# Transposing the normalized tokens of two chunks by DMA, adding the output bias on VectorE, and a new instruction order

## The chip, the cores and the metric

The kernel runs on one core of one Trainium2 chip. The metric is device time in microseconds of one execution, as the median of several runs. The profile that is read below is one execution of the same program; its span runs from the first to the last instruction, and the execution's own time is a little longer than its span.

## The reference, cut to what matters

Two layers read the same normalized tokens and their results are added to the input: a local attention with 32 heads of 20 channels, in which each token looks at itself and the seven tokens 2, 4, ... 14 places back, and a dense layer with a gelu in the middle.

```
x = A_x                              # 1 x 2048 x 640, bf16
xn = layernorm(x)
qkv = xn @ wqkv                      # 640 -> 3*640, heads of 20
logits[s, w] = q[s] . k[s - 2*w] / sqrt(20), w = 0..7   (masked below token 0)
A = (softmax(logits) applied to v[s - 2*w]) @ wo
B = gelu(xn @ w1 + b1) @ w2 + b2     # 640 -> 1536 -> 640
out = x + A + B
```

## The kernel before, in words

The 2048 tokens are cut into 4 chunks (n = 0 to 3) of 512 tokens, each of 4 blocks (bl) of 128 tokens. A chunk goes through these steps, named as in the planner:

- `st`, `rs`, `rc`: mean and variance of each token on VectorE, square root on ScalarE, reciprocal on VectorE.
- `xn`: the normalized block, 128 tokens x 640 channels, in one of 2 buffers. VectorE writes it for chunk 0, ScalarE for the others (L399).
- `tp`, `tc`: five 128x128 transposes of that block on TensorE into a PSUM tile of the pool `acc` (L417), and ScalarE's copy into the chunk's transposed tile `xnT` (L421), of which there are 3.
- `pj`, `pc` (for chunk 0 `gj`, `gc`): q, k and v by TensorE, and ScalarE's copies out of PSUM. `pad` copies 14 columns from the chunk before.
- `qk`, `lg`: eight products q*k shifted, on VectorE (L493), and their sums over each head's channels on TensorE (L505).
- `m`, `mx`, `ex`, `ss`, `ri`, `at`: the softmax, `ex` on ScalarE and the others on VectorE.
- `xd`, `xs`: the weights `attn` are spread to all channels (`ax`, one buffer) by two DMAs from SyncE and two from ScalarE (L572).
- `av`, `ad`, `ot`: eight products with v (L588), three sums (L597) and the last sum into `oT` (L603), on VectorE.
- `f1`, `ge`: the 12 tiles of the dense layer's first product on TensorE (L610) and the gelu on ScalarE (L621).
- `o`, `oc`, `od`: for each block five pieces on TensorE: pieces 0 to 3 multiply the gelu's tiles by `w2`, piece 4 multiplies `oT` by `wo`, all into the same two PSUM tiles `lo` (512 columns, L643) and `hi` (128 columns, L645). ScalarE copies them to one of 2 tiles `osb` (L650, L651), and a GpSimd DMA adds `osb` to the output in DRAM (L657).

The output in DRAM is first filled with x by one DRAM-to-DRAM DMA (L330). A GpSimd DMA then adds b2, broadcast to 128 rows (`b2bc`), to each block (L656), ahead of the block's own result. The last block is different: `xb` adds b2 to its x on VectorE (L427), a product with the identity adds that to PSUM, and its `lo` and `hi` parts are written without accumulation, from SyncE and from ScalarE (`oclo`, `ohi`, `ochi`).

PSUM tiles for `tp`, `pj`, `gj` and `f1` come from a pool of 4 (`acc`); so do `lo` and `hi` of every second block of the last chunk. The other blocks share one pair (`O`).

The order of the instructions is written out by a planner. Each step has an engine, a duration, a rank, the steps that it needs and the buffers that it holds. The planner plays this through in time: whenever an engine is free it starts the step with the lowest rank of those that are ready. The steps' functions are then called in the order of these starts, and each engine executes its instructions strictly in that order, waiting where the real data are late. DMAs are steps of a fourth engine, "dq", that does one at a time; the real queue is SyncE's. The table `RANK` holds offsets to the ranks, by the first three or four letters of a step's name.

```
early = base + (-37.0 if n == 1 else -85.0)          # base = n * 52
pl.add(f"pj{n}{which}{to}", PE, 1.08, r, ...)        # r = early, for v early + 20
pl.add(f"f1{n}{ft}", PE, 1.08, base + 10.0 + 1.0 * ft, ...)
pl.add(f"o{n}{bl}{pc}", PE, us, base + PERIOD + 8.0 + 8.0 * bl, ...)
pl.add("ohi", PE, 1.05, base + PERIOD + 90, ...)
```

Of the kernel before, what the change touches and what calls it, by code (L numbers as in the profile page):

```python
# [133 lines left out]
LASTB = S // P - 1  # L134
# [4 lines left out]


RANK = {
# [4 lines left out]
}  # L146


def make_plan(fns, offsets=RANK):

    pl = Plan(offsets)
# [6 lines left out]
    def f(kind, *a):  # L158
        return lambda: fns[kind](*a)

    def done(n, which):
        if n:
            return [f"pc{n}{which}{to}" for to in range(KT)]
        return [f"gc{bl}{g}" for bl in range(BPC) for g, parts in enumerate(GROUPS) if which in [p[0] for p in parts]]

    for n in range(NCH):
        base = n * PERIOD
        prev = base - PERIOD
        early = base + (-37.0 if n == 1 else -85.0)
        xnT, q, k, v, oT = (("xnT", n), ("q", n), ("k", n), ("v", n), ("oT", n))  # L170
# [10 lines left out]
            pl.add(f"rc{n}", VE, 0.25, early + -4.0, [f"rs{n}"], f("rstd", n, 0, BPC))  # L181
        for bl in range(BPC):
            xn, tp = ("xn", n, bl), ("acc", "tp", n, bl)
            pl.add(f"xn{n}{bl}", SE if n else VE, 0.65 if n else 0.42, early + -4.0 if n else -99, [f"rc{n}" if n else f"rc{n}{bl}"], f("xn", n, bl), [xn])
            pl.add(f"tp{n}{bl}", PE, 0.3, early + -3.0 if n else -99, [f"xn{n}{bl}"], f("tp", n, bl), [xn, tp])
            pl.add(f"tc{n}{bl}", SE, 0.65, early + -3.0 if n else -99, [f"tp{n}{bl}"], f("tc", n, bl), [tp, xnT])
        if n == NCH - 1:
            pl.add("xb", VE, 0.5, base + 36, [f"xn{n}{BPC - 1}"], f("xb"), after=31.0)

        if n == 0:  # L190
            for bl in range(BPC):
                for g, parts in enumerate(GROUPS):
                    ps, last = ("acc", "g", bl, g), max(p[0] for p in parts)
# [5 lines left out]
        for which, buf in enumerate((q, k, v)):  # L199
# [5 lines left out]
            if which:  # L205
                need = done(n - 1, which) if n else []
# [3 lines left out]
        L = ("L", n)  # L210
        for wp in range(W // 2):
            pr = ("prod", "qk", n, wp)
            for i in range(2):
                need = done(n, 0) + done(n, 1) + [f"pad{n}1"]
                pl.add(f"qk{n}{wp}{i}", VE, 1.42, base + 3.0 * wp + i, need, f("qk", n, wp, i), [q, k, pr])
            pl.add(f"lg{n}{wp}", PE, 0.6, n - 1000, [f"qk{n}{wp}{i}" for i in range(2)] + ([f"lg{n}{wp-1}"] if wp else []), f("lg", n, wp), [pr, L], slack=0.8)

        e, at, ax = ("e", n), ("attn", n), ("ax", n)
        m, rs, ss, z = ("m", n), ("rs", n), ("ss", n), ("prod", "z", n)
# [4 lines left out]
        pl.add(f"ri{n}", VE, 0.96, n - 1000, [f"ss{n}"], f("recip", n), [ss, rs])  # L224
        pl.add(f"at{n}", VE, 1.22, n - 1000, [f"ri{n}"], f("attn", n), [e, rs, at])
        pl.add(f"xs{n}", SE, 1.2, n - 1000, [f"at{n}"], f("xs", n), [at, ax])
        pl.add(f"xd{n}", DQ, 5.5, n - 1000, [f"at{n}"], f("xd", n), [at, ax])

        prs = [("prod", "av", n, wp) for wp in range(W // 2)]
        for wp in range(W // 2):  # L230
            for i in range(2):
                need = [f"xd{n}", f"xs{n}", f"pad{n}2"] + done(n, 2)
                pl.add(f"av{n}{wp}{i}", VE, 1.42, base + 15.0 + 6.0 * wp + i, need, f("av", n, wp, i), [v, ax, prs[wp]])
        for k2, (a, b, r) in enumerate(((0, 1, 9.0), (2, 3, 21.0), (0, 2, 22.0))):
            need = [f"av{n}{x}{i}" for x in (a, b) for i in range(2)] if k2 < 2 else [f"ad{n}0", f"ad{n}1"]
# [8 lines left out]
        for bl in range(BPC):  # L244
            ob = ("osb", n, bl)
            O = [("O", n, bl)] if n < NCH - 1 or bl % 2 == 0 else [("acc", "lo", n, bl), ("acc", "hi", n, bl)]
            final = n * BPC + bl == LASTB
            last = None
            for pc in range(5):
                need = [last] if last else [f"ge{n}{ft}" for ft in range(FT)] + (["xb"] if (n, bl) == (NCH - 1, BPC - 1) else [])  # L250
                if pc == 4:
                    need.append(f"ot{n}")
                us = (0.65, 0.65, 0.65, 0.87, 1.08)[pc] if final else (0.82, 0.82, 0.82, 0.82, 1.37)[pc]
                last = pl.add(f"o{n}{bl}{pc}", PE, us, base + PERIOD + 8.0 + 8.0 * bl, need, f("o", n, bl, pc, ("lo",) if final else ("lo", "hi")), O + (hTs if pc == 0 else hTs[3 * pc : 3 * pc + 3] if pc < 4 else [oT]), 31.0)
            if final:
                pl.add("oclo", SE, 0.55, base, [last], f("oclo"), O + [ob])
                last = pl.add("ohi", PE, 1.05, base + PERIOD + 90, [last], f("ohi"), O)
                pl.add("ochi", VE, 0.25, base, [last], f("ochi"), O + [ob])
                continue
            pl.add(f"oc{n}{bl}", SE, 0.78, base, [last], f("oc", n, bl), O + [ob])  # L260
            pl.add(f"od{n}{bl}", SE, 0.0, base, [f"oc{n}{bl}"], f("od", n, bl), [ob])
# [4 lines left out]
def kernel(  # L266
# [16 lines left out]
    nc = tc.nc  # L283
    assert tuple(A_x.shape) == (1, S, D) and tuple(B_w1.shape) == (D, F)

    x_sd = A_x.rearrange("b s d -> (b s) d")
    out_sd = out.rearrange("b s d -> (b s) d")
# [8 lines left out]
    xtp = ctx.enter_context(tc.tile_pool(name="xtp", bufs=3))  # L296
# [9 lines left out]
    x_sb = wts.tile([P, NCH * BPC, D], BF16, name="x_sb")  # L306
# [5 lines left out]
    b2bc = consts.tile([P, D], BF16, name="b2bc")  # L312
# [9 lines left out]
    for n in range(1, NCH):  # L322
        cs = slice(n * BPC, (n + 1) * BPC)
# [2 lines left out]
    nc.sync.dma_start(w2_sb[:], B_w2.rearrange("(t p) n -> p t n", p=P))  # L326
    nc.sync.dma_start(wo2[:], A_wo.rearrange("(p t) n -> p t n", t=KT))  # L327
    nc.sync.dma_start(b2bc[:], b2_bcast)  # L328

    nc.sync.dma_start(out_sd[0 : LASTB * P, :], x_sd[0 : LASTB * P, :])  # L330


    ident = consts.tile([P, P], BF16, name="ident")
# [31 lines left out]
    tiles = {}  # L365

    def get(key, make):
        if key not in tiles:
            tiles[key] = make()
        return tiles[key]  # L370
# [52 lines left out]
            tiles["tp", n, bl][:, 0 : KT * P].rearrange("p (t m) -> p t m", t=KT),  # L423
        )

    def do_xb():
        nc.vector.tensor_tensor(out=x_sb[:, LASTB, :], in0=x_sb[:, LASTB, :], in1=b2bc[:], op=ALU.add)  # L427


    def qkv_tile(n, which):  # L430
# [222 lines left out]
    def do_od(n, bl):  # L653
        b = n * BPC + bl
        rows = out_sd[b * P : (b + 1) * P, :]
        nc.gpsimd.dma_start(rows, b2bc[:], accum_op=ALU.add)  # L656
        nc.gpsimd.dma_start(rows, tiles["osb", n, bl][:], accum_op=ALU.add)  # L657


    last = (NCH - 1, BPC - 1)  # L660
# [18 lines left out]
    with tc.manual_schedule(engines=engines):  # L679

        idle = psA.tile([P, CH], F32, tag="acc", name="idle")
        for _ in range(WARM):
            nc.tensor.matmul(idle[:, 0:P], lhsT=ident[:], rhs=ident[:], start=True, stop=True)
        for t in make_plan(fns).run():
            t["fn"]()
# [30 lines left out]
```

## Time and profile before

| | |
|---|---|
| time, median of 3 runs | 227.08 us (226.92 to 228.39) |
| the profiled execution: its own time | 227.29 us |
| its span | 225.0 us |
| TensorE (PE) busy | 212.4 us, 94% |
| VectorE (DVE) busy | 175.3 us, 78% |
| ScalarE (ACT) busy | 115.7 us, 51% |
| GpSimd (POOL) busy | 27.8 us, 12% |
| mean granted TensorE clock | 0.995 |
| DMA traffic | 21.98 MB, mean 98 GB/s |

Names in the profile: PEld is TensorE's weight load; SPq, ACTq and POOLq are DMA issues from SyncE, ScalarE and GpSimd. A row of the timeline gives start and duration in us, engine, line, operation, output and inputs, the number of instructions, and in brackets the idle time of the engine before it and what ended it. Matmuls are pipelined: a row's duration reaches to the modelled end of its last one, so the cost of a run of matmuls is read from start to start.

### The profile page before, as it was taken

How to read it: one execution, taken by the hardware profiler on the slowest of the kernel's cores; microseconds unless marked ns; L12 is line 12 of the kernel's file. 1: busy time of each engine (PE TensorE's matmuls, PEld its weight loads, DVE VectorE, ACT ScalarE, POOL GpSimd, SP SyncE). 2: the span in 40 equal slices, each digit the busy share in tenths (PEclk: the TensorE clock that was granted, in tenths of full speed). 3: DMA queues.
4: the chain of work that ended last, by engine and by line, in shares of the span. 5: the costliest groups of instructions: out<-in, count | busy, mean ns of one | idle time of the engine just before them, and what ended most of it. 6: DMA issues, size and time to landing. Idle time of an engine off the chain costs nothing.

```text
span 225.0 us, 4057 instructions
## 1 busy us (share of the span) xinstructions
PE 212.4 (94%) x1728; PEld 123.2 (55%) x1754; DVE 175.3 (78%) x166; ACT 115.7 (51%) x203; POOL 27.8 (12%) x48
## 2 busy tenths in 40 slices
PE   6899999999996999999999999999999999999990
PEld 6799745555443555555555555555445455455550
DVE  3759997567399998999899999999998229995000
ACT  3675988887674746923277542221548431511220
POOL 2000004990000000101010001111100110101111
PEclk9999999999999999999999999999999999999998
DMA  6999992999300000227001422222200532202322
GB/s 228 366 368 389 378 468 42 155 171 198 92 0 0 3 0 0 32 39 179 0 3 26 97 92 29 29 32 31 32 0 0 109 110 29 29 3 29 54 29 35
DMA packets 13625, 21.98 MB, mean 98 GB/s; under 512 B 1144, under 2 KB 10744, under 8 KB 13560
## 3 DMA queue, kind: packets, MB, share of 16 engines
q1 hardware_dynamic: 7848, 14.52, 19.7%
q0 software_dynamic: 4320, 4.92, 16.9%
q10 hardware_dynamic: 1440, 2.29, 3.2%
q8 instruction: 13, 0.21, 0.4%
q14 instruction: 4, 0.03, 0.0%
HBM read 12.45 MB, written 7.54 MB: 89 GB/s over the span
## 4 chain that ended last, share of the span: by engine, by line
issue 71%; POOL 10%; SPq 9%; DMA 7%; POOLq 1%
DMA out_dram<-in_A_x_dram 7%; POOL out_dram L657 5%; POOL out_dram L656 5%; SPq L327 4%; SPq L324 2%; SPq L326 1%; SPq L325 1%; SPq L318 1%; SPq L321 0%; POOLq L711 0%; SPq L320 0%; SPq L328 0%; SPq L315 0%; POOLq L657 0%; POOLq L656 0%
## 5 line engine op out<-in xcount | busy, mean ns | idle before, releaser
L610 PE MATMUL hps<-xnT,w_sb 128*128 128x512 bf16 x234 | 55.2, 380 | 0.3
L588 DVE TENSOR_TENSOR pv<-vT,ax 128x2560 bf16<-128x2560 bf16 x32 | 45.9, 1485 | 12.2 <-DMA ax<-attn 12.1
L643 PE MATMUL lo<-w_sb,hT 128*128 128x512 bf16 x183 | 52.2, 380 | 0.0
L493 DVE TENSOR_TENSOR prod<-qT,kT 128x2560 bf16<-128x2560 bf16 x32 | 45.8, 1486 | 3.1 <-ACT kT L478 2.8
L621 ACT ACTIVATE hT<-hps,b1T 128x512 bf16<-128x512 f32 x48 | 31.9, 688 | 19.7 <-PE hps L610 14.4
L645 PE MATMUL hi<-w_sb,hT 128*128 128x128 bf16 x192 | 40.3, 219 | 0.6 <-issue 0.2
L610 PEld LDWEIGHTS <-w_sb 128*128 128x128 bf16 x240 | 22.4, 98 | 26.2 <-issue 1.5
L597 DVE TENSOR_TENSOR pv<-pv 128x5120 bf16<-128x5120 bf16 x12 | 33.8, 2822 | 0.2
L657 POOL DMA_DIRECT2D out_dram<-osb x15 | 12.9, 863 | 157.0 <-ACT osb L651 157.0
L650 ACT CAST osb<-lo 128x512 bf16<-128x512 f32 x15 | 8.8, 587 | 45.6 <-PE hi L645 29.6
L643 PEld LDWEIGHTS <-hT 128*128 128x128 bf16 x192 | 18.7, 98 | 22.5 <-issue 0.4
L643 PE MATMUL lo<-wo,oT 128*128 128x512 bf16 x76 | 22.4, 380 | 0.0
L645 PEld LDWEIGHTS <-hT 128*128 128x128 bf16 x192 | 18.3, 98 | 2.1
L656 POOL DMA_DIRECT2D out_dram<-b2bc x15 | 13.5, 2696 | 35.1 <-DMA out_dram<-in_A_x_dram 35.1
L443 PE MATMUL pps<-xnT,wq_sb 128*128 128x512 bf16 x72 | 17.5, 381 | 0.2
L443 PE MATMUL pps<-xnT,wk_sb 128*128 128x512 bf16 x74 | 17.3, 379 | 0.2
L645 PE MATMUL hi<-wo,oT 128*128 128x128 bf16 x80 | 16.9, 219 | 0.2
L443 PE MATMUL pps<-xnT,wv_sb 128*128 128x512 bf16 x72 | 16.7, 380 | 0.3 <-ACT xnT L421 0.2
L478 ACT CAST qT<-pps 128x512 bf16<-128x512 f32 x15 | 8.8, 588 | 11.5 <-PE pps L443 11.5
L505 PE MATMUL L<-prod,head_of 128*32 128x256 bf16 x320 | 11.7, 275 | 2.1 <-DVE prod L493 2.1
L376 DVE BATCH_NORM_STATS2 stats<-x_sb 128x6 f32<-128x320 bf16 x16 | 7.4, 462 | 7.1 <-DMA x_sb<-in_A_x_dram 7.1
L399 ACT ACTIVATE xn<-x_sb,nmr,rstd 128x640 bf16<-128x640 bf16 x12 | 10.8, 921 | 4.0 <-PE tp L417 4.0
(68 smaller groups left out, 217.2 us busy)
## 6 DMA issues: line engine op xcount, KB each, us to landing
w_sb<-in_B_w_dram SPq DMA_DIRECT2D x2, 1920.0 KB, 16.4
out_dram<-in_A_x_dram SPq DMA_DIRECT2D x1, 2400.0 KB
out_dram<-b2bc POOLq DMA_DIRECT2D x15, 160.0 KB, 7.3
out_dram<-osb POOLq DMA_DIRECT2D x15, 160.0 KB, 3.4
ax<-attn SPq DMA_DIRECT2D x8, 256.0 KB, 5.3
ax<-attn ACTq DMA_DIRECT2D x8, 256.0 KB, 6.6
x_sb<-in_A_x_dram SPq DMA_DIRECT2D x3, 640.0 KB, 11.4
wq_sb<-in_A_wqkv_dram SPq DMA_DIRECT2D x1, 800.0 KB, 4.7
```

Of the source, the lines that this page charges most:

```text
L399: nc.scalar.activation(xn[:], x_sb[:, b, :], ACT.Identity, bias=nmr[:, b : b + 1], scale=rstd[:, b : b + 1])
L443: nc.tensor.matmul(ps[:], lhsT=wqkv_p[which][:, ti, to, :], rhs=xnT[:, ti, :], start=(ti == 0), stop=(ti == KT - 1),)
L493: nc.vector.tensor_tensor(out=prod[:, i, :, :], in0=qkv_tile(n, 0)[:], in1=qkv_tile(n, 1)[:, :, off : off + CH], op=ALU.mult,)
L505: nc.tensor.matmul(L[j * H : (j + 1) * H, 2 * wp : 2 * wp + 2, :], lhsT=head_of[:], rhs=prod[:, :, t, j * P : (j + 1) * P], start=(t == 0 ...
L588: nc.vector.tensor_tensor(out=pv[:, i, :, :].rearrange("p t (j c) -> p t j c", j=BPC), in0=qkv_tile(n, 2)[:, :, off : off + CH].rearrange( ...
L597: nc.vector.tensor_tensor(out=ta[:], in0=ta[:], in1=tb[:], op=ALU.add)
L610: nc.tensor.matmul(ps[:], lhsT=w1_sb[:, ti, ft * P : (ft + 1) * P], rhs=tiles["xnT", n][:, ti, :], start=(ti == 0), stop=(ti == KT - 1),)
L621: nc.scalar.activation(hT[:], tiles["hps", n, ft][:], ACT.Gelu_apprx_tanh, bias=b1T[:, ft : ft + 1], scale=1.0)
L643: nc.tensor.matmul(lo[:], lhsT=lhs, rhs=rhs[:, 0:CH], start=first, stop=last)
L645: nc.tensor.matmul(hi[:, 0 : D - CH], lhsT=lhs, rhs=rhs[:, CH:D], start=first, stop=last)
L656: nc.gpsimd.dma_start(rows, b2bc[:], accum_op=ALU.add)
L657: nc.gpsimd.dma_start(rows, tiles["osb", n, bl][:], accum_op=ALU.add)
```

## The change

- The blocks of chunks 2 and 3 are no longer transposed on TensorE and copied by ScalarE. Each normalized block is transposed by one DMA from SyncE straight into `xnT` (`do_td`, a step of the engine "dq" with 4.0 us).
- The DRAM-to-DRAM copy of x and the GpSimd DMAs that add `b2bc` are gone. Instead VectorE adds b2 to the x of a whole chunk in one instruction of 128 x 2560 (`xb0` to `xb3`), and a DMA from SyncE writes the result to the output (without the last block). The `o` steps of a chunk need its `xb`.
- The offsets in `RANK` are others, and a few durations in the plan are changed, so the order is another.

```diff
 RANK = {
-    "ad01": -51.8, "ad02": -11.1, "ad22": 55.2, "av0": -75.4, "av1": -80.6, "av2": 15.4, "f10": 39.3, "f11": 0.8,
-    "f12": 46.1, "f13": 9, "ge1": -74.9, "gj3": 24.7, "o00": 64.8, "o01": 58, "o02": 58.8, "o21": 9.1,
-    "o30": 13.6, "o32": -88, "o33": -87.4, "pc10": 184.3, "pc12": -37.1, "pj21": -29.9, "qk1": -33.9, "qk2": -278.2,
-    "qk3": -4, "st2": 95.7, "tc1": -44.4, "tp2": 50.9, "tp3": -44.5, "xb": 57, "xn1": 17.4, "xn2": 19.4,
+    "ad00": 178, "av2": 376.9, "f11": 47.4, "f12": 101.9, "f13": 56.6, "gj1": 41.2, "gj3": 41.9, "o01": -41.2,
+    "o02": 33.3, "o13": 84.5, "o23": 46.4, "ot0": 75.1, "pc12": 58.9, "pj30": 33.5, "pj32": 57, "qk2": -89.4,
+    "st2": 250.4, "tc1": -2.9, "xb0": 48.2,
 }
...
-            pl.add(f"xn{n}{bl}", SE if n else VE, 0.65 if n else 0.42, early + -4.0 if n else -99, ...)
+            pl.add(f"xn{n}{bl}", SE if n else VE, 0.81 if n else 0.42, early + -4.0 if n else -99, ...)
+            if n > 1:
+                pl.add(f"tc{n}{bl}", DQ, 4.0, early - 3.0, [f"xn{n}{bl}"], f("td", n, bl), [xn, xnT])
+                continue
             pl.add(f"tp{n}{bl}", PE, 0.3, ...)
             pl.add(f"tc{n}{bl}", SE, 0.65, ...)
-        if n == NCH - 1:
-            pl.add("xb", VE, 0.5, base + 36, [f"xn{n}{BPC - 1}"], f("xb"), after=31.0)
+        pl.add(f"xb{n}", VE, 1.43, base + 36, [f"xn{n}{bl}" for bl in range(BPC)], f("xb", n), after=32.0)
...
-            pl.add(f"lg{n}{wp}", PE, 0.6, ...)
+            pl.add(f"lg{n}{wp}", PE, 0.65, ...)
-        pl.add(f"xd{n}", DQ, 5.5, ...)
+        pl.add(f"xd{n}", DQ, 6.0, ...)
...
-                need = [last] if last else [f"ge{n}{ft}" for ft in range(FT)] + (["xb"] if (n, bl) == (NCH - 1, BPC - 1) else [])
+                need = [last] if last else [f"ge{n}{ft}" for ft in range(FT)] + [f"xb{n}"]
...
-    nc.sync.dma_start(out_sd[0 : LASTB * P, :], x_sd[0 : LASTB * P, :])
...
-    def do_xb():
-        nc.vector.tensor_tensor(out=x_sb[:, LASTB, :], in0=x_sb[:, LASTB, :], in1=b2bc[:], op=ALU.add)
+    def do_td(n, bl):
+        xnT = get(("xnT", n), lambda: xtp.tile([P, KT, CH], BF16, tag="xnT", name="xnT"))
+        nc.sync.dma_start_transpose(xnT[:, :, bl * P : (bl + 1) * P], tiles["xn", n, bl][:])
+
+    def do_xb(n):
+        cs = slice(n * BPC, (n + 1) * BPC)
+        nc.vector.tensor_tensor(
+            out=x_sb[:, cs, :],
+            in0=x_sb[:, cs, :],
+            in1=b2bc[:].unsqueeze(1).to_broadcast([P, BPC, D]),
+            op=ALU.add,
+        )
+        cs = slice(n * BPC, min((n + 1) * BPC, LASTB))
+        nc.sync.dma_start(out_sd.rearrange("(b p) d -> p b d", p=P)[:, cs, :], x_sb[:, cs, :])
...
     def do_od(n, bl):
         b = n * BPC + bl
         rows = out_sd[b * P : (b + 1) * P, :]
-        nc.gpsimd.dma_start(rows, b2bc[:], accum_op=ALU.add)
         nc.gpsimd.dma_start(rows, tiles["osb", n, bl][:], accum_op=ALU.add)
```

More of the change, by code (lines that the diff above doesn't have):

```diff
@@ L183, in make_plan @@
             xn, tp = ("xn", n, bl), ("acc", "tp", n, bl)
-            pl.add(f"xn{n}{bl}", SE if n else VE, 0.65 if n else 0.42, early + -4.0 if n else -99, [f"rc{n}" if n else f"rc{n}{bl}"], f("xn", n, bl), [xn])
+            pl.add(f"xn{n}{bl}", SE if n else VE, 0.81 if n else 0.42, early + -4.0 if n else -99, [f"rc{n}" if n else f"rc{n}{bl}"], f("xn", n, bl), [xn])
+            if n > 1:
+                pl.add(f"tc{n}{bl}", DQ, 4.0, early - 3.0, [f"xn{n}{bl}"], f("td", n, bl), [xn, xnT])
+                continue
             pl.add(f"tp{n}{bl}", PE, 0.3, early + -3.0 if n else -99, [f"xn{n}{bl}"], f("tp", n, bl), [xn, tp])
             pl.add(f"tc{n}{bl}", SE, 0.65, early + -3.0 if n else -99, [f"tp{n}{bl}"], f("tc", n, bl), [tp, xnT])
-        if n == NCH - 1:
-            pl.add("xb", VE, 0.5, base + 36, [f"xn{n}{BPC - 1}"], f("xb"), after=31.0)
+        pl.add(f"xb{n}", VE, 1.43, base + 36, [f"xn{n}{bl}" for bl in range(BPC)], f("xb", n), after=32.0)
         if n == 0:
@@ L215, in make_plan @@
                 pl.add(f"qk{n}{wp}{i}", VE, 1.42, base + 3.0 * wp + i, need, f("qk", n, wp, i), [q, k, pr])
-            pl.add(f"lg{n}{wp}", PE, 0.6, n - 1000, [f"qk{n}{wp}{i}" for i in range(2)] + ([f"lg{n}{wp-1}"] if wp else []), f("lg", n, wp), [pr, L], slack=0.8)
+            pl.add(f"lg{n}{wp}", PE, 0.65, n - 1000, [f"qk{n}{wp}{i}" for i in range(2)] + ([f"lg{n}{wp-1}"] if wp else []), f("lg", n, wp), [pr, L], slack=0.8)
         e, at, ax = ("e", n), ("attn", n), ("ax", n)
@@ L226, in make_plan @@
         pl.add(f"xs{n}", SE, 1.2, n - 1000, [f"at{n}"], f("xs", n), [at, ax])
-        pl.add(f"xd{n}", DQ, 5.5, n - 1000, [f"at{n}"], f("xd", n), [at, ax])
+        pl.add(f"xd{n}", DQ, 6.0, n - 1000, [f"at{n}"], f("xd", n), [at, ax])
         prs = [("prod", "av", n, wp) for wp in range(W // 2)]
```

## The prediction

> **What bounds the kernel now.** I read the page's busy times first, then the busy times by stretch.
>
> ```profile
> span 225.0 us, 4057 instructions
> PE 212.4 (94%) x1728; PEld 123.2 (55%) x1754; DVE 175.3 (78%) x166; ACT 115.7 (51%) x203; POOL 27.8 (12%) x48
> ```
>
> ```profile
> 50.00:75.00 25.00, 22.67 (x159) 11.83 (x161) 19.39 (x13) 17.13 (x26) 0.53 (x1) 1.00 0.35 70
> 75.00:100.00 25.00, 24.59 (x189) 13.72 (x191) 24.07 (x17) 14.92 (x26) 0.86 (x1) 1.00 0.08 10
> ...
> 175.00:200.00 25.00, 24.84 (x148) 12.73 (x150) 16.90 (x11) 8.82 (x17) 2.59 (x3) 1.00 0.32 63
> ```
>
> In these rows the columns after the stretch's length are PE, PEld, DVE, ACT and POOL busy, then the granted clock. PE is busy for 24.59 to 24.84 of 25 us in six of the seven stretches from 25 to 200; in the other one (50 to 75) it idles for 2.33. A busy PE could still be a slow one, so I checked its pace in the timeline: 20 matmuls of 512 columns take 4.48 us, of which 0.38 is one matmul's whole duration, so (4.48 - 0.38) / 19 = 0.216 us each, and a tile of `f1` (five) 1.08 us. That pace holds wherever such runs stand.
>
> ```profile
> 174.35 4.48 PE L610 MATMUL hps<-xnT,w_sb 128*128 128x512 bf16 x20
> ```
>
> PE is therefore the bound from its first transpose to its last matmul. What a change is worth is (1) PE work that disappears, (2) PE idle time that disappears, and (3) the stretch after PE's last matmul.
>
> The one large idle time is found in the timeline, together with what made VectorE late:
>
> ```profile
> 37.05 13.49 POOL L656 DMA_DIRECT2D out_dram<-b2bc  x15 [35.09 <-DMA out_dram<-in_A_x_dram]
> 48.70 1.31 SPq L572 DMA_DIRECT2D ax<-attn  x2
> 59.87 8.50 DVE L588 TENSOR_TENSOR pv<-vT,ax 128x2560 bf16<-128x2560 bf16 x6 [4.11 <-DMA ax<-attn]
> 68.29 1.48 DVE L493 TENSOR_TENSOR prod<-qT,kT 128x2560 bf16<-128x2560 bf16 x1
> 69.83 0.73 PE L505 MATMUL L<-prod,head_of 128*32 128x256 bf16 x20 [2.06 <-DVE prod L493]
> 184.13 5.70 DVE L588 TENSOR_TENSOR pv<-vT,ax 128x2560 bf16<-128x2560 bf16 x4 [8.03 <-DMA ax<-attn]
> ```
>
> The first `ax` is issued at 48.70 and used at 59.87, 11.2 us later. The 15 DMAs that add `b2bc` are issued from 37.05 to 50.5, so they are in flight then. VectorE idles 4.11 us for `ax`; the product after these six is late by that, and PE waits 2.06 us for it.
>
> The end:
>
> ```profile
> 204.12 1.49 DVE L603 TENSOR_TENSOR oT<-pv 128x2560 bf16<-128x2560 bf16 x1
> 210.46 0.59 ACT L665 CAST osb<-lo 128x512 bf16<-128x512 f32 x1 [0.38 <-ACT osb L651]
> 211.07 0.35 SPq L666 DMA_DIRECT2D out_dram<-osb  x1
> 217.82 0.83 PE L645 MATMUL hi<-w_sb,hT 128*128 128x128 bf16 x12
> 218.54 0.44 PE L645 MATMUL hi<-wo,oT 128*128 128x128 bf16 x5
> 218.57 0.59 ACT L650 CAST osb<-lo 128x512 bf16<-128x512 f32 x1 [3.82 <-DMA out_dram<-osb]
> 219.40 0.36 ACTq L675 DMA_DIRECT2D out_dram<-osb  x1
> 219.62 0.86 POOL L657 DMA_DIRECT2D out_dram<-osb  x1 [3.71 <-ACT osb L651]
> ```
>
> ```profile
> out_dram<-osb POOLq DMA_DIRECT2D x15, 160.0 KB, 3.4
> ax<-attn SPq DMA_DIRECT2D x8, 256.0 KB, 5.3
> x_sb<-in_A_x_dram SPq DMA_DIRECT2D x1, 160.0 KB, 2.7
> out_dram<-osb SPq DMA_DIRECT2D x1, 128.0 KB, 3.1
> out_dram<-osb ACTq DMA_DIRECT2D x1, 32.0 KB, 1.5
> ```
>
> PE ends at 218.98 and the span at 225.0, 6.02 later. ScalarE's copy of the second last block waits for a free `osb` (3.82, until an accumulating DMA has landed), then GpSimd issues at 219.62; 3.4 us to landing gives 223.0, and 2.0 us of closing follow.
>
> **The change part by part.**
>
> *Transposes, chunks 2 and 3.* In the timeline these are the last eight groups of five at L417. I take each from its start to the next matmul's start:
>
> ```profile
> 64.88 0.72 PE L417 MATMUL tp<-ident,xn 128*128 128x128 bf16 x10
> 65.44 2.32 PE L610 MATMUL hps<-xnT,w_sb 128*128 128x512 bf16 x9
> 71.58 0.72 PE L417 MATMUL tp<-ident,xn 128*128 128x128 bf16 x10
> 72.14 0.38 PE L643 MATMUL lo<-w_sb,hT 128*128 128x512 bf16 x1
> 73.77 0.44 PE L417 MATMUL tp<-ident,xn 128*128 128x128 bf16 x5
> 74.26 1.24 PE L443 MATMUL pps<-xnT,wk_sb 128*128 128x512 bf16 x4
> 88.48 0.73 PE L417 MATMUL tp<-ident,xn 128*128 128x128 bf16 x10
> 89.05 0.38 PE L643 MATMUL lo<-wo,oT 128*128 128x512 bf16 x1
> 90.52 0.44 PE L417 MATMUL tp<-ident,xn 128*128 128x128 bf16 x5
> 91.11 1.24 PE L443 MATMUL pps<-xnT,wv_sb 128*128 128x512 bf16 x5 [0.15 <-ACT xnT L421]
> ```
>
> 0.56 + 0.56 + 0.49 + 0.57 + 0.59 = 2.77 us of PE, all of it on the bound. Without the short waits for ScalarE's copy (the 0.15 above, and what makes the single groups dearer than half of a pair) it is 8 x 0.28 = 2.2. I take **-2.8**, bounds -2.2 and -2.8. The eight copies that go from ScalarE lie beside PE's work (ACT 51%) and are counted at nothing.
>
> The Trainium skill, page "VectorE: DVE Perf Modes", section "The three transpose paths", puts a 128x128 transpose on TensorE at 390 ns. By it the 40 transposes would be worth 15.6 us and the kernel would come down to about 208 us. The trace shows 0.056 us each, start to start, so the measurement decides and the term stays at 2.8.
>
> ```profile
> 45.19 0.92 ACT L399 ACTIVATE xn<-x_sb,nmr,rstd 128x640 bf16<-128x640 bf16 x1
> ```
>
> *Eight DMA transposes on SyncE's queue.* None is in the trace. The nearest rows are the load of the same 160 KB, 2.7 us, and the SBUF-to-SBUF `ax` on the same queue, 5.3 us for 256 KB; the longest `ax` was the first one, 11.2 us from issue to use. I take 5.3, as the nearest row in both places and queue, with 2.7 and 11.2 as the ends. It adds two waits. TensorE's first projection of chunk 2 or 3 waits for the last transpose of that chunk, and everything on PE stands behind it; the trace normalizes chunk 2's first block at 45.19, while the first projection that reads it starts at 74.26, so some 29 us lie between against 4 x 5.3 = 21 if they run one by one. And `xn` has two buffers: on ScalarE the third block's `xn` waits for the first one's transpose, and so on, six such waits in all, with gelus and PSUM copies queued behind. The planner reserves 4.0 us for each, so at 5.3 a wait is 1.3 us. PE meanwhile has up to four `acc` tiles, 4 x 1.08 = 4.3 us of work. Cost at 5.3: **0**; if all six came in one run, 6 x 1.3 - 4.3 = 3.5. Behind a transpose that waits, SyncE's `ax` DMAs wait too; they are issued with VectorE's softmax, tens of us apart, and I count nothing.
>
> *Bias on VectorE.* An add of 128x2560 is priced by L603, 1.486 us; the single add of before goes:
>
> ```profile
> L603 DVE TENSOR_TENSOR oT<-pv 128x2560 bf16<-128x2560 bf16 x4 | 5.9, 1486 | 0.1
> L427 DVE TENSOR_TENSOR x_sb<-x_sb,b2bc 128x640 bf16<-128x640 bf16 x1 | 0.5, 486 | 0.0
> ```
>
> 4 x 1.486 - 0.486 = 5.46 us more on VectorE, which isn't the bound. It would become one if `oT` of the last chunk came too late. PE needs after that `oT` four pieces 4 (89.05 to 90.52 above: at most 1.47 each, 5.9) and pieces 0 to 3 of the one block that finds no PSUM before (12 pairs, 12/5 x 1.47 = 3.5): 9.4 us. Before, it had 13.4 (205.6 to 218.98). With PE ending at 214.1 (below), `oT` must be there at 204.7, 0.9 earlier than before and with 5.46 more work: VectorE must recover 6.4 us of its idle time. I see 4.1 in the first `ax` wait, whose cause goes (next part), and two adds, 3.0, that fit into waits: `xb3` ranks at 192, in the neighbourhood of the 8.03 us wait at 176. That is 7.1: enough, narrowly. Cost **0**.
>
> *Output DMAs.* The DRAM-to-DRAM copy and the 15 bias DMAs go; four writes of x come (640 KB each, 480 the last), spread over the run, issued from SyncE. The first `ax` then has no accumulations beside it, so the 4.11 us of VectorE and with them PE's 2.06 go: **-2.1**, bounds 0 (the new order puts a wait elsewhere, or a write of x stands ahead of an `ax` on the queue) and -2.3. The accumulation of a chunk's first block now waits for that chunk's write; two `osb` tiles cover it.
>
> *Order and tail.* Without the offsets on `o32` and `o33`, the ranks make `o33` (156 + 52 + 32 = 240) the last block, so its `lo`, then `hi`, end PE, and the accumulating blocks end at least a piece earlier. With T as PE's end: `hi` takes 1.16 (217.82 to 218.98); `lo` ends at T - 1.16, ScalarE starts 0.1 later, SyncE issues 0.61 after that (210.46 to 211.07), landing 3.1: T + 2.65, closing 2.0: T + 4.65, against T + 6.02 now: **-1.4**. Bounds: 0, and -2.1 if only the small write counts (T + 0.42 + 1.5 + 2.0).
>
> Sum: span 225.0 - 2.8 - 2.1 - 1.4 = 218.7, with PE ending at 218.98 - 2.8 - 2.1 = 214.1. The profiled execution took 227.29, 2.29 over its span, so 221.0 for its like; it lies 0.21 above the median of 227.08, which makes **220.8 us**.
>
> **The rivals.**
>
> *VectorE becomes the bound.* None of its `ax` waits is recovered: `oT` at 205.6 + 5.46 = 211.1, PE's end at 211.1 + 9.4 = 220.5, span 225.1, time 227.2. For it: DVE is busy 24.07 of 25 us from 75 to 100. Against it: 12.1 us of waits for `ax` in the two rows above.
>
> *Only the transposes count.* The stall moves and the end still hangs on an accumulation, so the searched order doesn't do what it says: 227.1 - 2.8 = 224.3. For it: nothing in the plan knows how long an accumulating DMA holds `osb`.
>
> *Slower: the transposes land late.* Place: the six `xn` on ScalarE. At 11.2 us each wait is 7.2 beyond the plan, less 4.3 of cover 2.9, six times 17.4: 238. If the six come together, so that PE's cover counts once, 6 x 7.2 - 4.3 = 38.9 would be the far end, and the point from which it decides falls from 4.0 + 4.3 + 6.3/6 = 9.4 to 4.0 + (4.3 + 6.3)/6 = 5.8 us. The planner spaces them, so I price it at 238 and go by 9.4. For it: nothing in this trace transposes by DMA. Against it: both nearest rows are under 5.4.
>
> The Trainium skill, in the section named above, gives 1309 ns for a 128x128 block through the DMA, an estimate of 6.5 us for five in a row; with the six excesses of 2.5 together and cover once that would be 220.8 + 15 - 4.3 = 231.5, and with the waits apart nothing. The Trainium skill, page "Advanced Engine Details and Errata", section "X-Bar Transpose (TRN2)", says that transposes are as fast as regular DMAs, which would leave the sum. No trace here shows a transpose by DMA yet.
>
> **How the numbers follow.** Forecast 0.60; VectorE bound 0.17; only the transposes 0.10; late transposes 0.13. 1% of this kernel is 2.3 us, about what its measurement can tell from no change. Faster by over 1% takes the forecast and most of the third case, 0.67; within 1% the second and the rest, 0.19; slower 0.14. The low end has all terms at their better bounds, 2.8 + 2.3 + 2.1, and half a us of PE's other idle time: 227.1 - 7.7 = 219.4, rounded down to 218.5 since the other stretches idle for up to 0.41 each. The high end holds the second case and a mild form of the last: 228.5.
>
> **What would show it.** PE's busy time 2 to 3 us lower; no PE wait over 1 us between 25 and 200; transposes landing under 6 us; the first `ax` used within 7 us of its issue; PE's end near 214 and the span's 4 to 5 later, after a write from SyncE. It is wrong if ScalarE's `xn` waits for transposes by several us and PE for PSUM behind it, if PE waits for `oT`, or if the writes of x delay `ax`.

## The result and the profile after

The changed kernel takes **218.65 us** (median of 4 executions, 218.45 to 218.93); the kernel before took 227.74 (226.92 to 230.62) beside it. The ratio is 0.961, with a 95% interval of 0.957 to 0.966: 3.9% faster, where I had forecast 2.8%; 218.65 lies just inside the low end of my range, 218.5. (The ratio leaves out the 230.62, a disturbed execution.) The changed kernel's profiled execution took 218.45, its span 216.7; against that of before (227.29 and 225.0) the span is 8.3 us shorter and the time 8.8.

First the page of the changed kernel (busy times), then its busy times by stretch, with the same columns as before.

```profile
span 216.7 us, 3977 instructions
PE 209.4 (97%) x1689; PEld 121.1 (56%) x1714; DVE 180.2 (83%) x169; ACT 110.6 (51%) x195; POOL 14.5 (7%) x33
```

```profile
50.00:75.00 25.00, 24.54 (x171) 12.44 (x174) 24.93 (x17) 16.29 (x25) 0.00 (x0) 1.00 0.45 109
75.00:100.00 25.00, 24.89 (x163) 13.34 (x164) 24.86 (x18) 13.27 (x23) 1.88 (x2) 1.00 0.28 68
...
175.00:200.00 25.00, 24.84 (x162) 13.33 (x165) 17.15 (x10) 6.33 (x14) 3.44 (x4) 1.00 0.17 21
```

PE's busy time fell by 3.0 us (212.4 to 209.4). The stretch from 50 to 75, where PE had idled for 2.33, now has 0.46 of idle time. (Part of the small idle times may be records that the profile lacks: it has 1689 matmuls for 1714 weight loads here, and 1728 for 1754 before. The kernel with TensorE's transposes back, below, has 1754 of each, and there PE is busy for 25.00 us in each of the four stretches from 100 to 200.) VectorE's busy time rose by 4.9, and it is nearly full from 50 to 100 (24.93 and 24.86); but from 175 on it has 8 us to spare, as before.

The timeline of the changed kernel around the stall of before, and where VectorE stands at the end:

```profile
34.77 2.89 DVE L432 TENSOR_TENSOR x_sb<-x_sb,b2bc 128x2560 bf16<-128x2560 bf16 x2
48.79 1.29 SPq L584 DMA_DIRECT2D ax<-attn  x2
56.76 8.49 DVE L600 TENSOR_TENSOR pv<-vT,ax 128x2560 bf16<-128x2560 bf16 x6
69.05 0.73 PE L517 MATMUL L<-prod,head_of 128*32 128x256 bf16 x20
198.11 1.49 DVE L615 TENSOR_TENSOR oT<-pv 128x2560 bf16<-128x2560 bf16 x1 [7.35 <-PE hi L657]
```

The six products that read `ax` start at 56.76 with no wait in brackets (before: 59.87, after 4.11 of waiting), and PE's logits at 69.05 have none either (before: 2.06). The last `oT` waits 7.35 us *for PE* (`oT` has one buffer, and PE's products still read it): VectorE is early, not late.

The DMA issues of the changed kernel (the last column is the median time to landing), and, from the answers for the tiles `xnT` and `ax`, the range of the landings of each, with that of `ax` in the kernel before as the third:

```profile
ax<-attn SPq DMA_DIRECT2D x8, 256.0 KB, 4.9
xnT<-xn SPq DMA_TRANSPOSE x8, 2.6
out_dram<-osb SPq DMA_DIRECT2D x1, 128.0 KB, 1.7
out_dram<-osb ACTq DMA_DIRECT2D x1, 32.0 KB, 1.5
```

```profile
DMA to landing us min/median/max: 2.6/2.6/5.6
```

```profile
DMA to landing us min/median/max: 4.0/5.3/7.0
```

```profile
DMA to landing us min/median/max: 4.0/5.9/10.3
```

```profile
58.56 0.92 ACT L398 ACTIVATE xn<-x_sb,nmr,rstd 128x640 bf16<-128x640 bf16 x1 [1.25 <-DMA xnT<-xn]
```

A block's DMA transpose lands in 2.6 us in the median (5.6 at most), half of what I had taken, and only one of the six `xn` that could wait for a transpose does so, for 1.25 us. The longest landing of an `ax` fell from 10.3 to 7.0 (the 11.2 of the prediction runs from the first issue to the use).

The end, in the timeline of the changed kernel:

```profile
211.04 0.86 POOL L668 DMA_DIRECT2D out_dram<-osb  x1 [3.76 <-ACT osb L663]
213.12 0.44 PE L657 MATMUL hi<-wo,oT 128*128 128x128 bf16 x5
213.25 0.36 SPq L677 DMA_DIRECT2D out_dram<-osb  x1
213.98 0.36 ACTq L686 DMA_DIRECT2D out_dram<-osb  x1
```

PE ends at 213.12 + 0.44 = 213.56 and the span 3.14 later (before: 6.02). The last accumulation is issued at 211.04, before PE's end; what ends the run is the small write of ScalarE at 213.98, which lands 1.5 later, at 215.5, and 1.2 us of closing.

So the span's 8.3 us are 5.4 of PE's end (218.98 to 213.56: 3.0 of busy time, 2.4 of idle time) and 2.9 of tail. A further 0.5 lies outside the span, 2.29 before and 1.75 after.

### The profile page after: what moved, and what is told of

The parts are those of the page before. It is cut to its first block, busy times and chain, and to the rows that moved or that the text cites. A ratio compares the mean times of both kernels' runs of the same rounds, so it can differ in the third digit from the quotient of the medians.

```text
span 216.7 us, 3977 instructions
## 1 busy us (share of the span) xinstructions
PE 209.4 (97%) x1689; PEld 121.1 (56%) x1714; DVE 180.2 (83%) x169; ACT 110.6 (51%) x195; POOL 14.5 (7%) x33
## 3 DMA queue, kind: packets, MB, share of 16 engines
q10 hardware_dynamic: 1440, 2.29, 3.1%
## 4 chain that ended last, share of the span: by engine, by line
PE 93%; DVE 1%; ACT 1%; DMA 1%; ACTq 1%; issue 1%; DVEq 0%
PE lo L655 27%; PE pps L455 23%; PE hps L622 22%; PE gps L472 8%; PE hi L657 8%; PE L L517 5%; DMA x_sb<-in_A_x_dram 1%; PE tp L416 1%; ACTq L584 1%; ACT L633 1%; DVE stats L375 0%; DVE stats L376 0%; ACT xnT L420 0%; ACT hT L633 0%; DVE xn L402 0%
## 5 line engine op out<-in xcount | busy, mean ns | idle before, releaser
L622 PE MATMUL hps<-xnT,w_sb 128*128 128x512 bf16 x230 | 53.2, 379 | 0.4
L655 PE MATMUL lo<-w_sb,hT 128*128 128x512 bf16 x187 | 52.9, 379 | 0.0
L633 ACT ACTIVATE hT<-hps,b1T 128x512 bf16<-128x512 f32 x48 | 31.4, 686 | 11.8 <-PE hps L622 9.8
L668 POOL DMA_DIRECT2D out_dram<-osb x15 | 13.1, 873 | 196.8 <-ACT osb L663 196.8
L455 PE MATMUL pps<-xnT,wv_sb 128*128 128x512 bf16 x74 | 17.3, 379 | 0.3 <-ACT hT L633 0.2
L455 PE MATMUL pps<-xnT,wq_sb 128*128 128x512 bf16 x72 | 16.7, 379 | 0.2
L490 ACT CAST vT<-pps 128x512 bf16<-128x512 f32 x15 | 8.7, 586 | 11.4 <-PE pps L455 9.4
L655 PEld LDWEIGHTS <-oT 128*128 128x128 bf16 x80 | 7.8, 98 | 9.6 <-issue 0.4
L455 PEld LDWEIGHTS <-wk_sb 128*128 128x128 bf16 x75 | 8.7, 118 | 7.3 <-issue 0.2
L455 PEld LDWEIGHTS <-wq_sb 128*128 128x128 bf16 x75 | 8.6, 118 | 7.1
L455 PEld LDWEIGHTS <-wv_sb 128*128 128x128 bf16 x75 | 8.5, 118 | 7.3 <-issue 0.5
## 6 DMA issues: line engine op xcount, KB each, us to landing
x_sb<-in_A_x_dram SPq DMA_DIRECT2D x3, 640.0 KB, 11.2
```

The source lines that it names most:

```text
L455: nc.tensor.matmul(ps[:], lhsT=wqkv_p[which][:, ti, to, :], rhs=xnT[:, ti, :], start=(ti == 0), stop=(ti == KT - 1),)
L622: nc.tensor.matmul(ps[:], lhsT=w1_sb[:, ti, ft * P : (ft + 1) * P], rhs=tiles["xnT", n][:, ti, :], start=(ti == 0), stop=(ti == KT - 1),)
L633: nc.scalar.activation(hT[:], tiles["hps", n, ft][:], ACT.Gelu_apprx_tanh, bias=b1T[:, ft : ft + 1], scale=1.0)
L655: nc.tensor.matmul(lo[:], lhsT=lhs, rhs=rhs[:, 0:CH], start=first, stop=last)
```

## The experiments

My theory after the result (A in the expectations): the transposes, the stall behind the bias accumulations and the tail each pay, as in the sum, and the new order only leaves room for them. The rival (B): the order itself does most, and the parts would matter little without it. The experiments undo parts within the new order, and do parts within the old one.

**The changed kernel again**, as a yardstick for the kernels that were timed with it.

> The changed kernel again, as the mark for the others on this chip. Every theory: 218.7 us within 0.5, that is 0.96 of the kernel before.

218.51 us (218.47 to 218.74), ratio 0.960 [0.956, 0.964]. It repeats to 0.1%.

**TensorE's transposes back, in the new order.**

```diff
-        nc.sync.dma_start_transpose(xnT[:, :, bl * P : (bl + 1) * P], tiles["xn", n, bl][:])
+        do_tp(n, bl)
+        do_tc(n, bl)
```

> The changed kernel with its order kept step for step, but each of the eight DMA transposes replaced, at its place in the order, by the five TensorE transposes and ScalarE's copy of before. Theory A (PE is the bound, and its work counts in full): 8 x 0.28 to 0.37 us come back, 2.2 to 3.0 us, so 220.9 to 221.7, with PE's busy time back at 212. Rival B (the new order has slack that hides them): 218.7, with PE idle time smaller instead. Over 222.5 would mean that ScalarE's copies or the shared PSUM tiles make PE wait, which neither counts.

222.44 us (222.24 to 222.68), ratio 0.977 [0.974, 0.981]: 3.9 us above the changed kernel, more than I had expected. The timeline of PE in this kernel shows a wait for the first copies, a typical group and the one dear one:

```profile
45.88 4.48 PE L456 MATMUL pps<-xnT,wk_sb 128*128 128x512 bf16 x20 [0.32 <-ACT xnT L420]
...
57.53 0.44 PE L416 MATMUL tp<-ident,xn 128*128 128x128 bf16 x5
57.81 0.38 PE L656 MATMUL lo<-w_sb,hT 128*128 128x512 bf16 x1
...
79.09 0.44 PE L416 MATMUL tp<-ident,xn 128*128 128x128 bf16 x5
80.32 2.32 PE L456 MATMUL pps<-xnT,wq_sb 128*128 128x512 bf16 x10 [0.78 <-ACT xnT L420]
```

Seven groups cost 0.28 us from start to start, as in my lower bound. The last costs 1.23, since PE waits 0.78 for ScalarE's copy of it. Together 7 x 0.28 + 1.23 = 3.2. The wait of 0.32 at 45.88, for ScalarE's copy of the second group, makes the 25 products with `wk_sb` 0.5 longer (5.88 us from their start to that of the next run, 5.40 in the changed kernel): 3.7. The last 0.2 is not in these rows. So 2.2 us are the transposes' own and about 1.4 are waits for the copies.

**Old output DMAs in the new order**: the DRAM copy of x and the 15 bias accumulations return, the adds on x and the chunk writes go.

```diff
+    nc.sync.dma_start(out_sd[0 : LASTB * P, :], x_sd[0 : LASTB * P, :])
...
+        if n == NCH - 1:
+            nc.vector.tensor_tensor(out=x_sb[:, LASTB, :], in0=x_sb[:, LASTB, :], in1=b2bc[:], op=ALU.add)
...
+        nc.gpsimd.dma_start(rows, b2bc[:], accum_op=ALU.add)
         nc.gpsimd.dma_start(rows, tiles["osb", n, bl][:], accum_op=ALU.add)
```

> The changed kernel with its order kept, DMA transposes kept, but the output filled as before: one DRAM-to-DRAM copy of x and fifteen GpSimd accumulations of b2, no bias add of a whole chunk on VectorE and no write of x from SyncE. Theory A (those DMAs make the first ax late, VectorE and then PE wait): the first ax is used about 11 us after its issue instead of 8, VectorE idles about 3 us there and PE some 2 us: 220.7. Rival B (PE has other work ready at that place in the new order): VectorE idles, PE does not, and the time stays at 218.7 within 0.5, or falls a little as VectorE has 5.5 us less to do.

Median 219.75 us, ratio 0.968 [0.962, 0.975]: 1.2 above the changed kernel. Three of the four executions took 219.56 to 219.79 at a granted clock of 1.000; the profiled one took 222.55 at 0.992. Its timeline and its busy times in steps of 2 us show the stall back, and what follows it:

```profile
71.33 0.73 PE L510 MATMUL L<-prod,head_of 128*32 128x256 bf16 x20 [2.03 <-DVE prod L498]
```

```profile
70.00:72.00 2.00, 0.67 (x21) 0.45 (x20) 2.00 (x2) 0.03 (x1) 0.00 (x0) 1.00 0.37 74
72.00:74.00 2.00, 2.00 (x11) 0.82 (x8) 2.00 (x1) 0.26 (x1) 0.00 (x0) 0.66 0.03 8
74.00:76.00 2.00, 2.00 (x6) 0.68 (x5) 1.97 (x3) 1.23 (x2) 0.00 (x0) 0.50 0.00 0
```

VectorE waited 4.2 us for `ax`, whose longest landing is 11.2 (before: 10.3). PE's wait is 2.03, as long as before's; after it the clock falls to 0.66 and 0.50 for 4 us, worth 2 x 0.34 + 2 x 0.50 = 1.7 of PE's time. Why the other three executions lie only 1.2 above the changed kernel, less than the wait, is not shown: none of them was profiled, and VectorE has 4.9 us less to do in this kernel.

**The changed kernel's code with the offsets of before** in `RANK`.

```diff
 RANK = {
-    "ad00": 178, "av2": 376.9, "f11": 47.4, "f12": 101.9, "f13": 56.6, "gj1": 41.2, "gj3": 41.9, "o01": -41.2,
...
+    "ad01": -51.8, "ad02": -11.1, "ad22": 55.2, "av0": -75.4, "av1": -80.6, "av2": 15.4, "f10": 39.3, "f11": 0.8,
...
```

> The changed kernel with the rank offsets of the kernel before, so only the parts are changed and the planner's order is close to the old one. Theory A (the parts carry the gain, the order only the tail): transposes 3.0 and the stall of 2.1 are gained, the old tail of 6 us stays: 227.2 - 5.1 = 222.1. Rival C (the searched order carries the gain): 224.5 or more.

236.5 us (236.32 to 236.82), ratio 1.039 [1.036, 1.043]: the rival's "224.5 or more" holds it, but neither theory had a kernel slower than the one before. In its timeline PE waits twice for the logits' products, and in the stretch from 75 to 100 it is busy for 15.62 us at a mean clock of 0.80:

```profile
80.50 1.26 PE L518 MATMUL L<-prod,head_of 128*32 128x256 bf16 x20 [3.71 <-DVE prod L506]
86.04 1.26 PE L518 MATMUL L<-prod,head_of 128*32 128x256 bf16 x20 [4.28 <-DVE prod L506]
```

```profile
75.00:100.00 25.00, 15.62 (x129) 8.63 (x128) 21.64 (x14) 4.79 (x8) 1.88 (x2) 0.80 0.32 74
```

The offsets belong to a set of steps. Put on another set they make an order that nobody chose, 18 us slower, so this run does not separate order from parts. The square of four runs further down does.

**Before, without the bias accumulations** (`b2` is left out of the fifteen accumulated blocks); the order stays.

```diff
-        nc.gpsimd.dma_start(rows, b2bc[:], accum_op=ALU.add)
         nc.gpsimd.dma_start(rows, tiles["osb", n, bl][:], accum_op=ALU.add)
```

> The kernel before with its order unchanged, but without the fifteen GpSimd accumulations of b2 (b2 is left out of those blocks). Theory A (these accumulations make the first ax late and so cost PE its 2.06 us): the first ax is used 6 to 7 us after issue instead of 11.2, VectorE's 4.1 us of idle time and PE's 2.06 go: 225.1. Rival B (PE's wait has another cause, or the time is given back later): 227.2 within 0.6. Rival D (the DRAM-to-DRAM copy is what delays ax): no change at ax either.

225.09 us (224.08 to 225.87), ratio 0.985 [0.978, 0.992]: 2.9 less than before beside it (227.99). Busy times from 50 to 75, and VectorE's only wait left for `ax`, that of the last chunk:

```profile
50.00:75.00 25.00, 24.73 (x172) 12.87 (x175) 22.15 (x14) 18.68 (x30) 0.00 (x0) 1.00 0.18 43
```

```profile
DVE pv L588 <- DMA ax<-attn: 8.4, 1, 8.4
```

PE's busy time there rises from 22.67 to 24.73, the whole of the wait. The accumulations did cause the stall.

**Before, with the last block last** (the offsets of `o32` and `o33` removed).

```diff
-    "o30": 13.6, "o32": -88, "o33": -87.4, "pc10": 184.3, ...
+    "o30": 13.6, "pc10": 184.3, ...
```

> The kernel before without the rank offsets of the blocks o32 and o33, nothing else, so that the last block, which is written without accumulation, comes last and the order before the end stays. Theory A (the tail hangs on which DMA is last): PE ends at 219.0 as before, the span 3.1 us later instead of 6.0: 224.3. Rival: an osb tile or the wait for oT holds PE up instead, and the time stays at 227.2 or rises.

Ratio 0.995 [0.990, 1.000]: no gain that can be measured; its executions scatter from 225.36 to 233.05. The tail did shrink as in the changed kernel: PE ends at 222.76 + 0.44 = 223.20, the span is 226.4, so 3.2 against 6.02. But PE ends 4.2 later. Its timeline, with the clock by stretches of 2 us:

```profile
70.43 1.26 PE L505 MATMUL L<-prod,head_of 128*32 128x256 bf16 x20 [2.35 <-DVE prod L493]
...
207.54 0.39 PE L643 MATMUL lo<-wo,oT 128*128 128x512 bf16 x1 [2.23 <-DVE oT L603]
...
222.76 0.44 PE L645 MATMUL hi<-wo,oT 128*128 128x128 bf16 x5
```

```profile
70.00:72.00 2.00, 1.57 (x21) 0.82 (x21) 2.00 (x2) 0.00 (x0) 0.00 (x0) 0.54 0.00 0
72.00:74.00 2.00, 2.00 (x12) 0.95 (x11) 1.97 (x2) 0.00 (x0) 0.00 (x0) 0.61 0.00 0
```

PE now waits 2.23 for the last `oT`; of the other 2.0 us by which it ends later, 1.5 are the lower clock after the wait at 70 us (1.57 x 0.46 + 2 x 0.39, from the two rows above) and 0.3 the longer wait there. That the early `o32` and `o33` had been the work that PE did while VectorE was late fits, and is not isolated. In this order the shorter tail was paid for by waits.

**Each DMA transpose issued twice, and four times**, in the changed kernel.

```diff
-        nc.sync.dma_start_transpose(xnT[:, :, bl * P : (bl + 1) * P], tiles["xn", n, bl][:])
+        for _ in range(2):   # 4 in the second kernel
+            nc.sync.dma_start_transpose(xnT[:, :, bl * P : (bl + 1) * P], tiles["xn", n, bl][:])
```

> The changed kernel with each DMA transpose done twice in a row into the same place, the second after the first has landed: the output is the same, each block lands after about 5.2 us instead of 2.6, the order is unchanged. The prediction's cover (4.0 us planned and 4.3 us of PSUM tiles, so it decides from 9.4 us on, or from 5.8 if the waits come together): 218.7 within 0.5. A rival without such cover (every us over the plan's 4.0 counts, six times): 226.

> The same with four transposes in a row, each block landing after about 10.4 us. Waits apart, each covered by 4.3 us: 6 x (10.4 - 8.3) = 12.6, so 231. Waits together, cover counted once: 6 x 6.4 - 4.3 = 34, so 253. If the tokens are transposed so early that even this is hidden: 219, or a few us more.

Twice: 218.76 us (218.65 to 218.9), ratio 0.957 [0.952, 0.963], as the changed kernel. Four times: 232.15 (230.2 to 233.6), ratio 1.016 [1.006, 1.025], 13.6 above it. The waits of ScalarE and of PE in the second kernel (total, times, longest), and its timeline:

```profile
ACT xn L398 <- DMA xnT<-xn: 19.1, 4, 10.7
PE hps L623 <- ACT vT L491: 6.2, 1, 6.2
PE hps L623 <- ACT hT L634: 3.3, 1, 3.3
```

```profile
55.23 19.23 SPq L429 DMA_TRANSPOSE xnT<-xn  x11
68.41 0.92 ACT L398 ACTIVATE xn<-x_sb,nmr,rstd 128x640 bf16<-128x640 bf16 x1 [10.69 <-DMA xnT<-xn]
```

The rival of late transposes is real, as a mechanism: ScalarE's `xn` waits for a transpose, and PE waits 6.2 and 3.3 us for the copy of `vT` and the gelu of `hT`, which are ScalarE's work behind it. The expectations of both runs took each transpose to be issued after the one before had landed; it is issued earlier. Here one takes SyncE 19.23 / 11 = 1.75 us with the gaps, and the last of four lands 2.6 us after its own issue, so a block's `xn` is held for some 3 x 1.75 + 2.6 = 7.9 us (an estimate from these rows), and with two for 1.75 + 2.6 = 4.4 at most. By my formula with spaced waits 7.9 costs nothing, since the plan and the cover make 8.3; by the one with the waits together it costs 6 x 3.9 - 4.3 = 19.1. With two, both formulas give nothing, as measured. The 13.6 speaks against the first and lies below the second. It is not cleanly the waits' either: PE waits 9.5 us in these two rows, and PE's clock was 0.978 in that execution.

**The new order with all the old parts**: TensorE's transposes and the old output DMAs, both edits of above at once.

> The order of the changed kernel, step for step, but both parts as before: TensorE transposes and ScalarE copies at the DMA transposes' places, and the output filled by the DRAM-to-DRAM copy and the GpSimd accumulations of b2. Theory A (order and parts add up): 218.5 + 3.9 + 1.2 from the two single undoings = 223.6, up to 226 where PE's wait of 2 us is followed by a lower granted clock; the order alone is then worth 3 to 4 us, nearly all of it in the tail. Rival (the order is worth nothing without the parts): 227.5.

223.45 us (222.98 to 223.87), ratio 0.979 [0.974, 0.985]. The waits of this kernel, then the end in its timeline (span 221.5):

```profile
DVE oT L609 <- PE hi L651: 7.3, 1, 7.3
DVE pv L594 <- DMA ax<-attn: 3.0, 1, 3.0
PE pps L449 <- ACT hT L627: 0.9, 1, 0.9
```

```profile
72.23 0.73 PE L511 MATMUL L<-prod,head_of 128*32 128x256 bf16 x20
...
217.79 0.44 PE L651 MATMUL hi<-wo,oT 128*128 128x128 bf16 x5
```

PE ends at 218.23, 0.75 earlier than before, and the tail is 3.27 instead of 6.02. The accumulations are still there and VectorE waits for `ax`, but only 3.0 us, and PE's logits do not wait: with the transposes to do, PE comes to them at 72.23, later than the 71.33 at which its wait ended with the old output DMAs alone. The order alone brings 2.1% of 227.7, 4.7 us (3.5 to 6.0 by the interval); by the profiled executions 2.75 of it is tail, 0.75 PE's end and 0.5 outside the span.

**The old order with the DMA transposes alone.**

```diff
     def do_tp(n, bl):
+        if n > 1:
+            return
...
+        if n > 1:
+            nc.sync.dma_start_transpose(xnT[:, :, bl * P : (bl + 1) * P], tiles["xn", n, bl][:])
+            return
```

> The kernel before, order kept step for step, with nothing changed but the transposes of chunks 2 and 3: no TensorE transposes, and a DMA transpose from SyncE where ScalarE's copy stood. PE's wait for VectorE and the old tail stay. Theory A: PE loses 8 x 0.28 to 0.37 us of work, 2.2 to 3.0: 224.5 to 225.3. Rival B (the time turns into longer waits, since PE still has to wait for VectorE at 69 us and for nothing else): 226 to 227.5, because transposes ahead of that wait only lengthen it.

Ratio 1.005 [1.000, 1.011]: no gain. SyncE's queue, VectorE and PE in its timeline:

```profile
46.49 3.95 SPq L424 DMA_TRANSPOSE xnT<-xn  x2
50.53 4.07 SPq L577 DMA_DIRECT2D ax<-attn  x2
...
63.42 8.50 DVE L593 TENSOR_TENSOR pv<-vT,ax 128x2560 bf16<-128x2560 bf16 x6 [7.28 <-DMA ax<-attn]
...
73.38 1.26 PE L510 MATMUL L<-prod,head_of 128*32 128x256 bf16 x20 [5.82 <-DVE prod L498]
```

The two transposes stand ahead of the first `ax` on SyncE's queue. It is issued at 50.53 instead of 48.70, VectorE waits 7.28 instead of 4.11 and PE 5.82 instead of 2.06. Beside the accumulations the longest transpose took 13.5 us to land, the longest `ax` 13.1. PE's clock then falls to 0.74, 0.50 and 0.91 in the three steps of 2 us from 72 to 78, which costs its busy time (0.62, 2.00 and 2.00) another 1.3 us. What PE no longer has to transpose is lost there.

**Chunk 1 by DMA as well**, with four `xn` buffers and offsets searched anew by the time that the planner computes. The transpose of the dense layer's biases is also called at another place, ahead of the second of chunk 0's projections instead of a fixed one.

```diff
-            if n > 1:
-                pl.add(f"tc{n}{bl}", DQ, 4.0, early - 3.0, ...)
+            if n > 0:
+                pl.add(f"tc{n}{bl}", DQ, 2.6, early - 3.0, ..., after=30.0 if n == 1 else 0.0)
```

> A version meant to beat the changed kernel: the second chunk is transposed by DMA too, four xn buffers instead of two, rank offsets chosen anew with the same planner (2.6 us planned for a DMA transpose, those of the second chunk not before 30 us, when the weights have landed). Theory A (PE is the bound): 4 x 0.28 to 0.3 us less PE work, 217.4. Rival (the transposes stand behind the weights' loads in SyncE's queue and land late, or PE waits in the new order): 219 or more.

225.47 us (224.87 to 226.74), ratio 0.990 [0.983, 0.997]: 7 us worse than the changed kernel, where 1.1 better was expected. Its timeline and its first stretch:

```profile
12.02 0.18 PE L353 MATMUL b_tp<-ident,b_rt 12*128 12x12 bf16 x1 [3.08 <-DMA b_rt<-in_B_b_dram]
```

```profile
0.00:25.00 25.00, 19.34 (x273) 18.73 (x274) 12.53 (x41) 11.48 (x28) 1.38 (x18) 0.93 0.98 340
```

PE came to the biases' transpose before their data had arrived, which the plan does not know, and lost 3.2 us of busy time in the first 25 (22.53 to 19.34). VectorE then waited 8.4 for the last `ax`. Whether chunk 1 by DMA is worth anything stays open; no version beat the changed kernel.

## Why the prediction was right, and where it was not

The four corners of one square, all in the new order, in us (the lower right one was timed later than the rest, on another chip):

| | new output DMAs | old output DMAs |
|---|---|---|
| transposes by DMA | 218.51 | 219.75 |
| transposes on TensorE | 222.44 | 223.45 |

Rows differ by 3.9 and 3.7, columns by 1.2 and 1.0. The times add up, on top of an order worth 4.7: 3.8 + 1.1 + 4.7 = 9.6, against 9.1 measured. The waits behind them do not: the old output DMAs make PE's logits wait 2.03 in the upper right kernel's profile and not at all in the lower right one's, where PE waits 0.9 for a gelu instead (0.20 with TensorE's transposes alone).

- **Transposes, forecast -2.8: about -3.8.** The kind of saving was right (PE work on the bound) and PE's busy time fell by 3.0. The term was mis-sized where it counted ScalarE's copies at nothing: in the new order eight groups on TensorE cost 8 x 0.28 = 2.2, my lower bound, and waits for the copies about 1.4. In the old order the DMA transposes alone gain nothing. The step "I count nothing" for SyncE's `ax` behind a transpose holds for the new order only.
- **The cost of the DMA transposes, forecast 0: about 0.** I took 5.3 us for a landing and 2.6 was measured; the bound below, the load of the same 160 KB with 2.7, was the better row. Twice the transposes cost nothing, four times 13.6, so the deciding point lies between some 4.4 and 7.9 us for which a block's `xn` is held. I went by the spaced one (9.4), which is too high by this; the lower one (5.8) fits. The estimate of 6.5 us from the Trainium skill, page "VectorE: DVE Perf Modes", section "The three transpose paths", does not agree with the 2.6 measured here; the rule of the Trainium skill, page "Advanced Engine Details and Errata", section "X-Bar Transpose (TRN2)", as fast as regular DMAs, does agree, with 2.6 beside 2.7.
- **The stall, forecast -2.1: gone, but not by the output DMAs alone.** The cause was named rightly: without the accumulations the wait vanishes in the old order. In the new order the old output DMAs bring back VectorE's wait for `ax`, and in one profile PE's 2.03, but in time they cost only 1.0 to 1.2, half of the forecast; why not all of it is not shown.
- **The tail, forecast -1.4: -2.9.** This is the term that I mis-sized. I gave the write from SyncE 3.1 us, from the row of the same write of before, and 2.0 of closing: T + 4.65. Here the write lands in 1.7 and the closing is 1.2. In the rows of before that write was issued 0.7 us after an accumulation (210.37, in the timeline), here 2.2 us after one (211.04). The other profiles agree: 2.9 to 3.0 in the three more kernels where an accumulation is issued 0.7 before the write (b2 left out, the old order with DMA transposes, the old offsets on the new code), 1.7 in the seven more where it is 2.2. No run changes this distance alone, so the cause is likely, and not shown. The bound that I had called "only the small write counts" is what happened: 0.42 from PE's end to ScalarE's issue, 1.5 to landing, 1.2.
- **VectorE as the bound: refuted.** VectorE was ready for the last `oT` 7.35 us before it could write it. I had looked for 6.4 us of recovered waits and called it narrow. The first two adds were placed at 34.77, and no `ax` wait was left at all.
- **What would show it.** PE's busy time (-3.0), no PE wait over 1 us, transposes under 6 us, PE's end near 214 (213.56): all seen. Two marks missed: the span ended 3.1 after PE, not 4 to 5, and the first `ax` was used 8.0 us after its issue, not within 7, because VectorE still had five products to finish and did not need it earlier.
- **Not counted: the clock after a stall.** Executions of before ran at a mean clock of 0.981 to 0.998, those of the changed kernel at 0.998 to 1.000. In before's own profile the clock stayed at 1.00 through its stall, so my sum against that execution had nothing to gain there; an execution of before at 0.986 took 229.84, 2.5 us longer than it.
- **Not explained:** the time outside the span, 2.1 us or more in every execution of before and 1.7 to 1.9 in the changed kernel. It is 1.74 also with all the old parts in the new order and 1.82 with the old offsets on the new code, but 2.18 in the old order with the last block last or with the DMA transposes. No run says why.

Of 9.1 us measured, then: 8.3 of span (my 6.3, and 1.5 of tail and 0.5 of PE's end more), 0.5 outside it, and the rest is before's median lying above its profiled execution. Two things in this are luck. The transposes' term was 1.0 too small and the stall's about 1.0 too large, so that their sum of 4.9 is the measured one. And the better bounds of my terms end at 219.4, above the 218.65: the range holds it because I rounded down to 218.5 for the small idle times of PE, part of which may be missing records.

## What to carry to other kernels

When a kernel is bound by one engine almost everywhere, price a change in three places: that engine's work, its waits, and the stretch after its last instruction; and take the price of a transfer from a row with the same neighbours: a spread of 256 KB took up to 10.3 us to land beside accumulating DMAs and 5.3 in the median of SyncE's eight. A change that gains nothing in one order (the DMA transposes, the last block last) can pay in another that leaves it slack; a 2 x 2 of runs in one order gives the worth of each part, and the corner with all the old parts that of the order. Offsets searched for one set of steps need not serve another (here they cost 18 us), and a plan that lacks a real wait (a DMA's arrival, a held buffer) can find an order that runs into it.

## What the runs showed that I had not expected

A stall of PE costs more than its length, in some executions. In two kernels a wait of 2.03 and 2.35 us is followed by about 4 us at a granted clock of 0.50 to 0.66 (the rows by 2 us above); in before a wait of 2.06 is followed by full speed:

```profile
70.00:72.00 2.00, 2.00 (x33) 1.20 (x26) 2.00 (x1) 0.00 (x0) 0.00 (x0) 1.00 0.00 0
72.00:74.00 2.00, 2.00 (x23) 1.29 (x21) 1.97 (x3) 1.88 (x3) 0.00 (x0) 1.00 0.00 0
```

The kernel with the old output DMAs took 219.56 to 219.79 us in three executions with the clock at 1.000, and 222.55 in the one with 0.992. The Trainium skill, page "TensorE: Matmul & The Clock Gate", in its section "Why this matters for your kernels", warns of idle gaps above about 3 us. The runs go below that: the lower clock followed gaps of 2.03 and 2.35 us in two profiles, and not the gap of 2.06 in a third. The kernels with waits of 3.7 to 5.8 us (the old offsets on the new code, the DMA transposes in the old order) all had mean clocks of 0.99 or less. A change that removes a bound engine's only long wait may thus gain more than the wait, and make the times steadier: 218.45 to 218.93 here, against 226.53 to 229.62 in the thirteen executions of before that were timed beside the kernel without the bias accumulations.
